# Six places of a fused attention and MLP kernel re-ordered

## The chip, the cores and the metric

The kernel runs on one core of a Trainium2 chip. The metric is the device time of one execution in microseconds (us). The engines are named as in the profile: PE (TensorE, matmuls), PEld (its weight loads), DVE (VectorE), ACT (ScalarE), POOL (GpSimd) and SP (SyncE, which here only issues transfers). Each engine works through its own queue in order and waits at an instruction until what that instruction needs is there; everything queued behind it waits too.

## The reference

Two branches read the same input `x` of 2048 tokens by 576 columns (32 heads of 18 columns), and their results are added to it. In the first, a token attends to itself and to seven earlier tokens, two apart. The second mixes neighbouring tokens, and then has an MLP of width 4608.

```python
def A(xn, wqkv, wo):                      # W, dil = 8, 2
    q, k, v = heads(xn @ wqkv)
    logits = einsum("bhsd,bhswd->bhsw", q, k[idx]) * scale   # idx = pos - 2 * (0..7), masked below 0
    return merge(einsum("bhsw,bhswd->bhsd", softmax(logits), v[idx])) @ wo

def B(x, w1, w2, w3, w4):
    h = gelu(layernorm(x) @ w1)
    x1 = x + shifted(h) @ w2              # four column blocks shifted by +1, -1, +2, -2 tokens
    return x1 + gelu(layernorm(x1) @ w3) @ w4

xn = layernorm(x)
return x + A(xn, wqkv, wo) + B(xn, w1, w2, w3, w4)
```

## The kernel before

Everything is float32. Each product is made from operands split in two parts: a *hi* part, a copy that ACT casts to the matmul's input type (fp32r), and a *lo* part, the difference between the value and hi, which DVE computes. `split_*`, `cast_*`, `hi_main`, `lo_main`, `signed` and `low_part` are these steps, for weights, for transposed tokens, for gelu results. A cast by ACT is therefore nearly always followed by a difference on DVE that reads ACT's result, and PE needs both.

The order of the instructions on each engine is the order in which the Python code emits them. Waits between engines follow from which tile is read or written, and a tile that is used again waits until its earlier users are done. The stages, in order of time:

**Prologue** (up to 24 us). The first four tiles of 128 tokens (t = 0 to 3) are normalized, turned by PE into a PSUM tile (`turn_x`, L333; the last columns by `turn_tail`, L302) and cast out of it (`cast_x`, L337: ACT L311 and DVE L312 for the main part, ACT L316 and DVE L317 for the tail). `q_part` (L388) issues matmuls n0 to n1 of the 14 of a tile's first product, `q_tail` the last two, and `q_leave`, which takes the result out. `split_cg(3)` splits the second block of weights, `rawb`, that later products use. The tiles are done in turn, and "unit 4", the first product with the second block, follows.

**Steps of q, k and v** (to about 192 us). Blocks p = 3 to 7 are made by a Strassen-like scheme, seven products of sums instead of eight. Each p has numbered slots, and a plan says which side work is emitted after which slot. `z_turn(t)` (L556) scales a tile on ACT (L558) and turns it on DVE (L129, L130); `put` stores the turned block. The matmuls are in `seven` (L593); `leave` (L601) takes a product out, with a copy on ACT or an addition on DVE (L608).

**The mixing branch** (to about 310 us), then **units** u = 0 to 23 (to about 613 us). A unit is a quarter of the tokens by 256 of the MLP's width: two `up` products (L1128, matmuls L1132, gelu on ACT L1114, low part on DVE L1126) and four `down` products of the unit before. A `down` (L1159, matmuls L1168) has twelve matmuls in a PSUM tile. The result leaves in one of three ways: a copy on ACT (L1173) and an accumulating transfer by POOL for tiles in `YD`; for a *seeded* tile, where the running sum was copied into PSUM beforehand by ACT (`ahead`, L1149), a copy back by ACT (L1176); otherwise an addition on DVE (L1179). `begin_downs` takes the list of tiles with their flag for seeds. There are two PSUM tiles, and `ahead` prepares the next as soon as one is out. `split_n(b, ...)` (L899) makes the signed hi and lo parts of the normalized block b, after `get_n` has read it by transfer (ACT L906 and following).

**Groups** q = 0 to 23 (to about 1197 us). The rest of the MLP is again Strassen-like. A group has seven products P1 to P7 (matmuls L1430), eight downs D0 to D7 of the group before, and side work. `ORDER` and `ORDERS` give the order of these fifteen items; `at(item, f, ...)` puts `f` behind an item. P3 gives, by the addition `z_add` (L1440), the value whose gelu is `c12` (`gelu12`, L1120; `low12`, L1126); P7 gives `c22` (`gelu22`, `low22`). `combine` (L1260, DVE L1265) makes four sums of weights in place, `split_a` and `split_s` split weights and their sums for the products of the next group, `split_op` the tokens' operands, `load_pair` and `load_w4` read weights. NWP is 12: groups 0 to 11 work on one half of the tokens, 12 to 23 on the other.

The attention runs through units and groups as background work on DVE and ACT. It is a generator; `bg(us, late)` (L1081) is called after each item and takes operations from it, for as much time as the item's other work on DVE (`spent`) has left. With `late` it also emits a pending exponential (`exp_now`). In group 18, behind P4, a loop takes all that is left.

**End.** The eight downs of the last group, then the output product `mm_tok` (L180, matmuls L183), for which `split_wo` splits the weights, and the stores.

Of the kernel before, what the change touches and what calls it, by code (L numbers as in the profile page):

```python
# [8 lines left out]
F32 = mybir.dt.float32  # L9
F32R = mybir.dt.float32r  # L10
AF = mybir.ActivationFunctionType
ALU = mybir.AluOpType
# [24 lines left out]
NPL = 6  # L37
# [20 lines left out]
def fused_block(ctx, tc, x, wqkv, wo, w1, w2, w3, w4, out):  # L58
# [393 lines left out]

    def q_head(t):
        pq[t] = psa.tile([128, 512], F32, name="p1", tag="a")
        q_part(pq[t], t, 0, 0, 12)

    def q_tail(t):
# [20 lines left out]
    q_tail(0)  # L478
    q_tail(1)
    pq[2] = psa.tile([128, 512], F32, name="p1", tag="a")  # L480
    q_part(pq[2], 2, 0, 0, 6)
    turn_tail(2, turns[2])
    cast_x(2, True)
    q_part(pq[2], 2, 0, 6, 12)
    turn_x(3)
    cast_x(3)
    turn_tail(3, turns[3])
    cast_x(3, True)
    q_tail(2)
    split_cg(3)  # L490
    q_head(3)
    q_tail(3)
# [163 lines left out]
    for p in range(3, 8):  # L656
# [6 lines left out]
        if n < 8:  # L663
            q4 = 4 * (p - 3)
            for k, t in zip({3: (9, 11, 14, 17), 6: (9, 11, 12, 14)}.get(p, (9, 12, 16, 18)),
                            (q4 + 1, q4 + 2, q4 + 3, q4) if p == 4 else range(q4, q4 + 4)):
                at(k, z_turn, t)
            at({3: 17, 6: 14}.get(p, 18), put, ("z", p - 3))
            if p > 3:
                at(0, norm_x, 2 * n + 1)  # L670
                at(0, tails, 2 * n + 1)
                at(2, stats_x, 2 * n)
            at(3, low2, n)
            at(4, norm_x, 2 * n)
            at(4, tails, 2 * n)
            at(7, up2, n)
            at(8, lambda n=n: cast_upper(n, two[n]))
            if n < 7:
                at(11, stats_x, 2 * n + 3)
            at(14, cast_s, n, 0)  # L680
            at(15, cast_s, n, 1)
            at(15, cast_s, n, 2)
            if p == 3:
                for t, k in enumerate((9, 11, 14)):
                    at(k, away, t, t + 1)
                at(11, scales, 4, 6)
                at(18, load_x, 13)
                at(18, load_x, 12)
            if p == 4:
                for t, k in ((5, 9), (6, 12), (7, 16)):  # L690
                    at(k, away, t, t + 1)
                at(18, away, 3, 5)
                at(11, scales, 8)
                at(12, scales, 10)
                at(18, load_x, 15)
                at(18, load_x, 14)
            if p == 5:
                at(11, load_w1)
                at(11, scales, 12)
            if p == 6:  # L700
                at(5, scales, 14)
        else:
            at(3, lambda: get(("z", 0), ring_block(("z", 0))))
            at(13, lambda: split_x(xring["z", 0], 2))
            at(15, lambda: split_x(xring["z", 0], 3))
            at(18, open_w1)
            at(18, split_w1, 0)
            at(20, lambda: split_x(xring["z", 0], 1))
# [190 lines left out]
    def split_n(b, xt, part=None, scr=None):  # L899
# [3 lines left out]
        vec = KV[:, b % 2:b % 2 + 1] if b % 2 == 0 else KV[:, 1:2]  # L903
        if part != 1:
            r = xt[:, 9, :] if scr is None else scr.bitcast(F32R)
            act.activation(r[64:128], raw[64:128, 4, :], AF.Identity, scale=k2)  # L906
            act.activation(xt[0:64, 4, :], raw[0:64, 4, :], AF.Identity, scale=k2)
            signed(xt[64:128, 4, :], raw[64:128, 4, :], k2, r[64:128])
            act.activation(xt[:, 0:2, :], raw[:, 5:7, :], AF.Identity, scale=k1)
            signed(xt[:, 5:7, :], raw[:, 5:7, :], k1, xt[:, 0:2, :])  # L910
        if part != 0:
            for k, sg in ((2, vec), (3, k2)):
# [346 lines left out]

    def combine(q):  # L1260
        spent[0] += 2.2
        st = WS["st", q]
        for o, i, op in ((1, 0, ALU.subtract), (0, 2, ALU.add), (2, 1, ALU.subtract),
                         (3, 2, ALU.subtract)):
            dve.tensor_tensor(st[:, :, o, :], st[:, :, o, :], st[:, :, i, :], op=op)  # L1265
# [43 lines left out]
    for u, (c, b) in enumerate(units):  # L1309
# [18 lines left out]
        for i in range(C):  # L1328
# [12 lines left out]
            if (u, i) == (3, 0):  # L1341
                pool.dma_start(yd[13], Y[:, 13, :])
                pool.dma_start(yd[15], Y[:, 15, :])
            if (u, i) in ((1, 0), (2, 1)):
                split_n(u + 1, x1n[u + 1], 0, RT)
# [17 lines left out]
        for j, (t, parts) in enumerate(prev):  # L1363
# [6 lines left out]
            if (u, j) == (3, 1):  # L1370
                next(state["gen"])
            if u in (1, 2) and j == 1:
                split_n(u + 1, x1n[u + 1], 1, RT)
            for f in {(-3, 1): (lambda: split_a(0),), (-3, 2): (lambda: split_w4(NPL),),
# [31 lines left out]
        if u in XADD:  # L1406
            add_x(XADD[u])
    close_ab()


    qpcc = tc.tile_pool(name="qpc", bufs=1, space=PSUM, reuse_waits="tile")
    qpc = qpcc.__enter__()
    qpdc = tc.tile_pool(name="qpd", bufs=1, space=PSUM, reuse_waits="tile")
    qpd = qpdc.__enter__()
    begin_downs([(4 * units[NU - 1][1] + j, False) for j in range(4)]
                + [(8 * (g // NWP) + (j + 4) % 8, g + 1 not in (NWP - 1, NWP))
                   for g in range(2 * NWP) for j in range(8)], 2,
                lambda n: qpd.tile([128, 2, 512], F32, name=f"ps{n % 2}"))
    Z1, Z2, Z3, Z4 = temp(13), temp(15), temp(5), temp(7)
    NQ = 2 * NWP  # L1420
    SLOT = {"A11": 0, "A22": 1, "A12": 2, "S1": 0, "S3": 1, "S2": 2, "S4": 3}
# [20 lines left out]
    def downs(g):  # L1442
        s0 = 8 * (g // NWP)
        w1, w0 = W4[2 * (NPL + pair(g))], W4[2 * (NPL + pair(g)) + 1]
        for j in range(8):
            if j < 4:
                yield lambda j=j: down(s0 + 4 + j, [(hid[g, "c12"], w0), (hid[g, "c22"], w1)])
            else:
# [36 lines left out]
    def o_turn(t):  # L1485
# [4 lines left out]
    ORDER = "P1 D0 P2 P6 D1 P5 D2 P7 D3 P4 D4 P3 D5 D6 D7"  # L1490
    ORDERS = {0: "P1 P2 D0 P6 P5 P7 D1 D2 P4 D3 P3",
              NWP - 1: "P1 D0 P2 P6 P5 P7 D1 P4 P3 D2 D3 D4 D5 D6 D7",
              NWP: "D0 D1 P1 D2 P2 P6 D3 P5 P7 D4 P4 P3 D5 D6 D7"}
    spent[0] = 0.0
    for q in range(NQ):
# [36 lines left out]
        if q == 0:  # L1532
            at("P6", split_op, 0, "T4")
            at("D1", gelu22)
            at("P7", split_a, n, (0, 1))
            at("D1", split_op, 0, "B22")
            at("D1", split_a, n, (2,))
            at("D2", low22)
            at("P3", gelu12)
            at("P3", combine, n)  # L1540
            at("P3", low12)
            at("P3", split_s, n, (0, 1))
            at("P3", split_s, n, (2,))
            at("P3", load_pair, q + 2)
        elif q == NWP - 1:
# [16 lines left out]
        elif q == NWP:  # L1562
# [10 lines left out]
            at("P7", split_a, n, (2,))  # L1573
            at("P7", combine, n)
            at("D4", gelu22)
            at("P4", low22)
            at("D5", gelu12)
            at("D5", split_s, n, (0, 1))
            at("D6", low12)
            at("D6", split_s, n, (2,))  # L1580
            at("D7", load_pair, q + 2)
# [15 lines left out]
        else:  # L1597
# [4 lines left out]
            at("D6", low12)  # L1602
            for k, it in enumerate(("P4", "D4", "P3", "D5", "D6")):
                at(it, split_wo, k)
# [7 lines left out]
        if z < -1 and q + 1 != NWP:  # L1612
            at("D5" if q else "P3", load_w4, NPL + pair(q + 1), 0)
        if 0 < q < 9:
# [13 lines left out]
        for it in ORDERS.get(q, ORDER).split():  # L1628
# [40 lines left out]
            for f in plan.get(it, ()):  # L1669
                f()  # L1670
            if z < -6 or z == -6 and EV[0]:
                bg(1.5 - spent[0], it == "P6" and q != NWP - 1)
                spent[0] = 0.0
# [96 lines left out]
```

## Time and profile before

| | |
|---|---|
| median of 3 runs | 1276.82 us (1276.55 to 1279.03) |
| profiled execution | 1276.11 us |
| its span | 1274.3 us |
| PE busy | 1256.3 us (99%) |
| DVE busy | 930.9 us (73%) |
| ACT busy | 765.7 us (60%) |
| POOL busy | 267.9 us (21%) |

In the timeline a row gives the start, the duration, the engine, the line and operation, the output and inputs by the program's names, the shapes, and how many instructions are run together in the row (x). A bracket at its end is the time that the engine stood idle just before, and what released it. In a row of windows there are, after the stretch's length, the busy time of PE, PEld, DVE, ACT and POOL with their instructions, then the granted clock of PE, the share of the transfers' engines, and GB/s.

### The profile page before, as it was taken

The page shows a single profiled execution, that of the slowest core. Times are in us where ns is not written, and L with a number is a line of the kernel's source. Part 1 is how long each engine was busy: PE and PEld are TensorE (multiplying, and loading weights), DVE is VectorE, ACT ScalarE, POOL GpSimd, SP SyncE. Part 2 cuts the span into 40 slices and gives each one's busy share as a digit, 9 for nine tenths or more (in the row PEclk, how much of TensorE's full clock was granted, in tenths as well). Part 3 has the DMA queues.
Part 4 walks back from the last instruction along what each step waited for, and adds up shares of the span by engine and source line. Part 5 has one row for each costly group of instructions (what it writes and reads, how often), then busy time and mean ns, then how long its engine had stood idle before and what let it go on. Part 6 is the DMA issues. An engine that isn't in the chain of part 4 may idle for free.

```text
span 1274.3 us, 21006 instructions
## 1 busy us (share of the span) xinstructions
PE 1256.3 (99%) x7819; PEld 1157.6 (91%) x7819; DVE 930.9 (73%) x1204; ACT 765.7 (60%) x1277; POOL 267.9 (21%) x408
## 2 busy tenths in 40 slices
PE   8999999999999999999999999999999999999998
PEld 8999998899898999999899999998888999898998
DVE  7877645688558989997659998889889883464341
ACT  4455557526645545455777767776677776677730
POOL 2213200021222211212123232222122222222200
PEclk9999999999999999999999999999999999999999
DMA  7638994446878986859669889788968769899972
GB/s 220 155 85 200 224 196 146 149 137 190 203 223 181 221 164 137 162 130 252 120 144 209 189 179 217 179 168 209 249 99 188 144 117 197 182 215 211 267 244 84
DMA packets 208654, 228.92 MB, mean 180 GB/s; under 512 B 80920, under 2 KB 142328, under 8 KB 208424
## 3 DMA queue, kind: packets, MB, share of 16 engines
q1 hardware_dynamic: 175800, 160.79, 44.7%
q0 software_dynamic: 32752, 66.80, 32.5%
q8 instruction: 61, 1.00, 0.3%
q14 instruction: 41, 0.34, 0.1%
HBM read 127.71 MB, written 110.23 MB: 187 GB/s over the span
## 4 chain that ended last, share of the span: by engine, by line
PE 64%; issue 3%; ACT 2%; DVE 2%; DMA 1%; POOL 0%; DVEq 0%; POOLq 0%; ACTq 0%
PE ps L1168 31%; PE cc L1430 19%; PE p L1132 10%; PE ps L183 4%; DMA yd<-Y 1%; DVE xt L897 0%; DVE w3st L1265 0%; POOL yd L1174 0%; ACT Y L1173 0%; PE p L1737 0%; ACT xt L1227 0%; ACT Y L1115 0%; DVE c L1126 0%; DVE Y L1179 0%; ACT c L1120 0%
## 5 line engine op out<-in xcount | busy, mean ns | idle before, releaser
L1168 PEld LDWEIGHTS ps<-w,c 128*128 128x128 f32 x3456 | 479.0, 189 | 22.2 <-ACT Y L1173 2.0
L1168 PE MATMUL ps<-w,c 128*128 128x288 f32 x3456 | 490.0, 297 | 6.2 <-ACT ev L1173 1.5
L1174 POOL DMA_DIRECT2D yd<-Y x154 | 138.0, 899 | 396.3 <-ACT Y L1173 332.0
L1126 DVE TENSOR_TENSOR c<-Y,c 128x512 fp32r<-128x512 f32 x144 | 98.8, 687 | 93.2 <-ACT Y L1115 91.8
L1173 ACT COPY Y<-ps 128x576 f32<-128x576 f32 x154 | 97.8, 636 | 77.2 <-PE ps L1168 66.7
L1430 PE MATMUL cc<-xt,w3s 128*128 128x512 f32 (+1 forms) x504 | 127.7, 393 | 0.9 <-DVE Y L1440 0.9
L1430 PEld LDWEIGHTS cc<-xt,w3s 128*128 128x128 f32 (+1 forms) x504 | 92.2, 188 | 19.1 <-DVE Y L1440 1.4
L1176 ACT COPY Y<-ps 128x576 f32<-128x576 f32 x92 | 58.9, 640 | 66.7 <-PE ps L1168 65.2
L1430 PE MATMUL cc<-x1n,w3a 128*128 128x512 f32 (+1 forms) x336 | 86.4, 396 | 0.3 <-ACT cc L1633 0.3
L1046 DVE TENSOR_TENSOR po<-q,k 128x1152 f32<-128x1152 f32 (+1 forms) x48 | 84.3, 1755 | 0.8
L1049 DVE TENSOR_REDUCE L<-po 128x64 f32<-128x1152 f32 (+1 forms) x48 | 84.0, 1751 | 0.8
L1114 ACT ACTIVATE c<-p 128x512 fp32r<-128x512 f32 x48 | 28.6, 597 | 84.9 <-PE p L1132 84.9
L1440 DVE TENSOR_TENSOR Y<-cc,Y 128x512 f32<-128x512 f32 x49 | 33.7, 688 | 58.9 <-ACT Y L1436 54.5
L1022 DVE TENSOR_TENSOR po<-v,L 128x1152 f32<-128x1152 f32 x56 | 75.4, 1354 | 0.9
L393 PE MATMUL p<-wb,xt 128*128 128x288 f32 (+1 forms) x504 | 71.2, 299 | 1.0 <-ACT stg L398 0.9
L1430 PEld LDWEIGHTS cc<-x1n,w3a 128*128 128x128 f32 (+1 forms) x336 | 61.2, 190 | 11.8 <-ACT cc L1633 0.5
L393 PEld LDWEIGHTS p<-wb,xt 128*128 128x128 f32 (+1 forms) x504 | 67.8, 189 | 2.4 <-ACT stg L398 1.3
L1026 DVE TENSOR_TENSOR po<-po 128x1152 f32<-128x1152 f32 x49 | 66.4, 1355 | 0.9
L597 PE MATMUL ca<-wb,xt 128*128 128x288 f32 x420 | 61.6, 297 | 1.5 <-DVE keep L608 1.5
L1149 ACT COPY ps<-Y 128x576 f32<-128x576 f32 x92 | 59.4, 646 | 4.4 <-DVE Y L1179 2.4
L597 PEld LDWEIGHTS ca<-wb,xt 128*128 128x128 f32 x420 | 57.6, 189 | 2.2 <-DVE keep L608 2.0
L113 POOL TENSOR_TENSOR rs<-rs,mhalf 128x1 f32<-128x1 f32 x32 | 19.4, 606 | 189.7 <-DVE mv L116 109.4
(256 smaller groups left out, 2146.9 us busy)
## 6 DMA issues: line engine op xcount, KB each, us to landing
yd<-Y POOLq DMA_DIRECT2D x156, 288.0 KB, 6.1
Y<-in_B_w_dram SPq DMA_DIRECT2D x29, 576.0 KB, 6.0
w3st<-in_B_w_dram SPq DMA_DIRECT2D x56, 256.0 KB, 8.0
qkvd<-stg SPq DMA_DIRECT2D x66, 144.0 KB, 3.3
yd<-ev POOLq DMA_DIRECT2D x26, 288.0 KB, 6.8
w3st<-in_B_w_dram SPq DMA_DIRECT2D x92, 64.0 KB, 7.8
xd<-st SPq DMA_DIRECT2D x16, 320.0 KB, 5.0
xd<-big SPq DMA_DIRECT2D x16, 320.0 KB, 7.1
```

What stands on the lines that cost most here:

```text
L393: pe.matmul(ps[:, :QB], xo[:n, o + k, a, :], W[:n, w + k, v, :], start=i == 0, stop=i == len(PLAIN) - 1)
L597: pe.matmul(ps[:, :QB], xo[:n, XO[x], a, :], W[:n, OP[w], v, :], start=start and i == 0, stop=stop and i == len(HALVES) - 1, skip_group_ch ...
L1022: dve.tensor_tensor(dst, vv, Lf[:, :, w:w + 1].to_broadcast([128, TPP * GH, HD]), op=ALU.mult)
L1026: dve.tensor_tensor(o, o, dst, op=ALU.add)
L1046: dve.tensor_tensor(dst, qf[:, None, :].to_broadcast([128, n, TPP * GC]), win, op=ALU.mult)
L1049: dve.tensor_reduce(Lw[:, w:w + n, :], dst.rearrange("p w (x d) -> p w x d", d=HD), axis=AX.X, op=ALU.add)
L1126: dve.tensor_tensor(h[:, 1, :], g, h[:, 0, :].bitcast(F32), op=ALU.subtract)
L1132: pe.matmul(ps, W3[f][:, w, :], x1n[b][:, a, :], start=n == 0, stop=n == len(PAIRS) - 1)
L1168: pe.matmul(ps[:, k, :HF], h[:, col], w[:, p, k * HF:(k + 1) * HF], start=n == 0 and not seed, stop=n == len(seq) - 1, skip_group_check=True)
L1173: act.copy(e.rearrange("p (h c) -> p h c", h=2), ps[:, :, :HF])
L1174: pool.dma_start(yd[t], e, accum_op=ALU.add)
L1430: pe.matmul(ps, WX[w][:k, v, SLOT[w], :], area[sb][xk][:k, a, :], start=onto is None and i == 0, stop=last and i == len(HALVES) - 1, skip_ ...
```

## The change

It moves work in six places; no matmul is added or removed.

1. In the prologue, `split_cg(3)` is taken apart: its hi and lo parts are emitted between the casts of tiles 2 and 3, the rest behind the tail cast of tile 3. `q_tail(2)` and the first six matmuls of tile 3 come ahead of `turn_tail(3)`.
2. For p = 6, the third and fourth `z_turn` go from slots 12 and 14 to 13 and 15, the `put` from 14 to 15.
3. `split_n` gets two more parts: 2 is the block's tail (with its lo), 3 the first two main pieces. For unit 2's block these and part 1 are emitted behind the downs 0, 1 and 2 of unit 1, where part 0 had stood behind the first `up` and part 1 behind down 1. Unit 3's block stays as it was.
4. In group 0, P3 comes ahead of D3, and the side work is placed anew, with `combine` in two halves.
5. In group 12, `combine` and `split_s` are halved in another place, and `bg` is skipped behind P6; the pending exponential is emitted behind P3 instead.
6. The last group's eight downs have no seeds (three of them had), and `split_wo` is spread differently. In addition the first four downs of all groups take `c22` first and `c12` second.

```diff
+    r3, o3 = qraw[3], OP["B12"]
     pq[2] = psa.tile([128, 512], F32, name="p1", tag="a")
     q_part(pq[2], 2, 0, 0, 6)
+    hi_main(r3, 0, o3, 0)
     turn_tail(2, turns[2])
     cast_x(2, True)
+    hi_main(r3, 0, o3, 1)
+    lo_main(r3, 0, o3, 0)
     q_part(pq[2], 2, 0, 6, 12)
     turn_x(3)
     cast_x(3)
+    q_tail(2)
+    lo_main(r3, 0, o3, 1)
+    pq[3] = psa.tile([128, 512], F32, name="p1", tag="a")
+    q_part(pq[3], 3, 0, 0, 6)
     turn_tail(3, turns[3])
     cast_x(3, True)
-    q_tail(2)
-    split_cg(3)
-    q_head(3)
+    split_tail(r3, 0, o3)
+    q_part(pq[3], 3, 0, 6, 12)
     q_tail(3)
...
-            for k, t in zip({3: (9, 11, 14, 17), 6: (9, 11, 12, 14)}.get(p, (9, 12, 16, 18)),
+            for k, t in zip({3: (9, 11, 14, 17), 6: (9, 11, 13, 15)}.get(p, (9, 12, 16, 18)),
...
-            at({3: 17, 6: 14}.get(p, 18), put, ("z", p - 3))
+            at({3: 17, 6: 15}.get(p, 18), put, ("z", p - 3))
...
-        if part != 1:
+        if part not in (1, 3):
             r = xt[:, 9, :] if scr is None else scr.bitcast(F32R)
...
+        if part not in (1, 2):
             act.activation(xt[:, 0:2, :], raw[:, 5:7, :], AF.Identity, scale=k1)
             signed(xt[:, 5:7, :], raw[:, 5:7, :], k1, xt[:, 0:2, :])
-        if part != 0:
+        if part not in (0, 2, 3):
...
-    def combine(q):
-        spent[0] += 2.2
+    def combine(q, n0=0, n1=4):
+        spent[0] += 0.55 * (n1 - n0)
...
-                         (3, 2, ALU.subtract)):
+                         (3, 2, ALU.subtract))[n0:n1]:
...
-            if (u, i) in ((1, 0), (2, 1)):
+            if (u, i) == (2, 1):
                 split_n(u + 1, x1n[u + 1], 0, RT)
...
-            if u in (1, 2) and j == 1:
-                split_n(u + 1, x1n[u + 1], 1, RT)
+            if u == 1 and j < 3:
+                split_n(2, x1n[2], (2, 3, 1)[j], RT)
+            if (u, j) == (2, 1):
+                split_n(3, x1n[3], 1, RT)
...
-                + [(8 * (g // NWP) + (j + 4) % 8, g + 1 not in (NWP - 1, NWP))
+                + [(8 * (g // NWP) + (j + 4) % 8, g + 1 not in (NWP - 1, NWP, NQ))
...
-                yield lambda j=j: down(s0 + 4 + j, [(hid[g, "c12"], w0), (hid[g, "c22"], w1)])
+                yield lambda j=j: down(s0 + 4 + j, [(hid[g, "c22"], w1), (hid[g, "c12"], w0)])
...
-    ORDERS = {0: "P1 P2 D0 P6 P5 P7 D1 D2 P4 D3 P3",
+    ORDERS = {0: "P1 P2 D0 P6 P5 P7 D1 D2 P4 P3 D3",
...
         if q == 0:
-            at("P6", split_op, 0, "T4")
+            at("D0", split_op, 0, "T4")
+            at("P6", split_op, 0, "B22")
+            at("P7", split_a, n, (0, 1))
             at("D1", gelu22)
-            at("P7", split_a, n, (0, 1))
-            at("D1", split_op, 0, "B22")
             at("D1", split_a, n, (2,))
-            at("D2", low22)
+            at("D1", combine, n, 0, 2)
+            at("D2", combine, n, 2, 4)
+            at("P3", split_s, n, (0,))
             at("P3", gelu12)
-            at("P3", combine, n)
-            at("P3", low12)
-            at("P3", split_s, n, (0, 1))
-            at("P3", split_s, n, (2,))
-            at("P3", load_pair, q + 2)
+            at("P3", low22)
+            at("D3", low12)
+            at("D3", split_s, n, (1, 2))
+            at("D3", load_pair, q + 2)
...
-            at("P7", combine, n)
+            at("P7", combine, n, 0, 2)
+            at("D4", combine, n, 2, 4)
             at("D4", gelu22)
             at("P4", low22)
             at("D5", gelu12)
-            at("D5", split_s, n, (0, 1))
+            at("D5", split_s, n, (0,))
             at("D6", low12)
-            at("D6", split_s, n, (2,))
+            at("D6", split_s, n, (1, 2))
...
-            for k, it in enumerate(("P4", "D4", "P3", "D5", "D6")):
+            for k, it in enumerate(("P4", "D4", "P3", "P3", "D7")):
                 at(it, split_wo, k)
...
-            at("D5" if q else "P3", load_w4, NPL + pair(q + 1), 0)
+            at("D5" if q else "D3", load_w4, NPL + pair(q + 1), 0)
...
-            if z < -6 or z == -6 and EV[0]:
-                bg(1.5 - spent[0], it == "P6" and q != NWP - 1)
+            if (z < -6 or z == -6 and EV[0]) and (q, it) != (NWP, "P6"):
+                bg(1.5 - spent[0], it == "P6" and q != NWP - 1 or (q, it) == (NWP, "P3"))
```

More of the change, by code (lines that the diff above doesn't have):

```diff
@@ L451, in fused_block @@
     pq = {t: psa.tile([128, 512], F32, name="p1", tag="a") for t in range(2)}
-    def q_head(t):
-        pq[t] = psa.tile([128, 512], F32, name="p1", tag="a")
-        q_part(pq[t], t, 0, 0, 12)
     def q_tail(t):
@@ L1408, in fused_block @@
     close_ab()
+    NQ = 2 * NWP
     qpcc = tc.tile_pool(name="qpc", bufs=1, space=PSUM, reuse_waits="tile")
@@ L1419, in fused_block @@
     Z1, Z2, Z3, Z4 = temp(13), temp(15), temp(5), temp(7)
-    NQ = 2 * NWP
     SLOT = {"A11": 0, "A22": 1, "A12": 2, "S1": 0, "S3": 1, "S2": 2, "S4": 3}
```

## The prediction

> **What bounds the kernel now.** I read the page's first two lines, then the timeline of TensorE (PE) filtered for idle in front of an instruction, then for each such idle the other engines' rows around it.
>
> ```profile
> span 1274.3 us, 21006 instructions
> PE 1256.3 (99%) x7819; PEld 1157.6 (91%) x7819; DVE 930.9 (73%) x1204; ACT 765.7 (60%) x1277; POOL 267.9 (21%) x408
> ```
>
> PE is busy all but 1274.3 - 1256.3 = 18.0 us, and the change removes no matmul. Only those 18 us, and matmuls that run slowly, can be won. An edit that makes ACT or DVE shorter where PE does not wait is worth nothing. So I looked where PE stands still in the six places:
>
> ```profile
> 18.28 0.41 PE L304 MATMUL ps<-ident,stg 128*128 128x128 f32 x2 [1.49 <-DVE xt L312]
> 165.66 0.54 PE L597 MATMUL ca<-wb,xt 128*128 128x288 f32 x2 [1.09 <-DVE keep L608]
> 329.90 1.87 PE L1168 MATMUL ps<-w,c 128*128 128x288 f32 x12 [1.49 <-ACT ev L1173]
> 634.39 0.80 PE L1168 MATMUL ps<-w,c 128*128 128x288 f32 x4 [0.87 <-ACT c L1120]
> 636.57 2.13 PE L1168 MATMUL ps<-w,c 128*128 128x288 f32 x8 [1.39 <-DVE c L1126]
> 920.91 1.88 PE L1430 MATMUL cc<-xt,w3s 128*128 128x512 f32 x7 [0.95 <-DVE Y L1440]
> 924.82 3.46 PE L1168 MATMUL ps<-w,c 128*128 128x288 f32 x24 [0.42 <-DVE Y L1179]
> 930.11 1.86 PE L1168 MATMUL ps<-w,c 128*128 128x288 f32 x12 [0.21 <-ACT ps L1149]
> 1197.05 5.20 PE L1168 MATMUL ps<-w,c 128*128 128x288 f32 x36 [0.50 <-ACT ps L1149]
> 1203.14 8.26 PE L1168 MATMUL ps<-w,c 128*128 128x288 f32 x60 [0.90 <-ACT Y L1173]
> 337.98 6.55 PE L1168 MATMUL ps<-w,c 128*128 128x288 f32 x48
> ```
>
> The brackets of the ten sum to 9.31 us. A stall costs a little more than its bracket: twelve matmuls of a down take 6.55/4 = 1.64 us in a stream, but 1.87 between two breaks, so 0.23 us drains at each. Ten stalls are worth 9.31 + 10 x 0.23 = 11.6 us. One more item (product or down) is 1.6 us; I use that pitch below.
>
> **Part 1, fourth tile's tails.**
>
> ```profile
> 16.77:19.90 3.13, 1.64 (x14) 1.65 (x14) 1.11 (x2) 1.76 (x4) 0.00 (x0) 1.00 0.02 5
> 16.82 0.58 ACT L311 CAST xt<-ps 128x512 fp32r<-128x512 f32 x1 [0.88 <-PE ps L300]
> 17.44 0.69 DVE L312 TENSOR_TENSOR xt<-ps,xt 128x512 fp32r<-128x512 f32 x1 [1.04 <-ACT xt L311]
> 18.73 0.37 ACT L316 CAST xt<-ps 96x256 fp32r<-96x256 f32 x1 [1.32 <-PE ps L304]
> 19.13 0.42 DVE L317 TENSOR_TENSOR xt<-ps,xt 32x256 fp32r<-32x256 f32 x1 [1.00 <-ACT xt L316]
> 18.45 2.64 PE L393 MATMUL p<-wb,xt 96*128 96x288 f32 x18
> ```
>
> The tail transposes wait until ACT's cast and DVE's difference have read their PSUM tile (18.13); then 2 + 12 + 2 matmuls at 2.64/18 = 0.147 us follow, to about 20.7. The change puts q_tail(2) and the first six of tile 3 (8 x 0.147 = 1.2 us), which need only the cast's end at 17.40, into the gap; what precedes them still waits to 17.44. The transposes keep 18.3. Behind them six matmuls end near 19.5, and the last two need the tail's difference, which ends at 19.55. Tile 3 ends at 19.9: **0.8 us** (0.3 if the weight casts, moved into ACT's 0.88 and 1.32 us holes, push the tail's casts; 1.1 if nothing waits).
>
> **Part 2, z turns.**
>
> ```profile
> 163.17 0.27 DVE L130 STREAM_TRANSPOSE st<-z 128x128 f32<-128x128 f32 x1
> 164.36 0.71 DVE L129 STREAM_TRANSPOSE st<-z 128x512 f32<-128x512 f32 x1 [0.93 <-ACT z L558]
> 165.19 0.42 DVE L608 TENSOR_TENSOR keep<-ca,keep 128x288 f32<-128x288 f32 x1
> ```
>
> The addition L608 stands in DVE's queue behind the transposes of slot 12's z turn, which themselves wait 0.93 us for ACT. Moved to slot 13 they come after it; the addition can follow 163.17 + 0.27, ends at about 163.9, and the stall goes: 1.09 + 0.23 at most, of which I take **1.25** (0.6 if ACT's later queue, one slot fuller, delays a copy). The `put` is one slot later on SP; nothing waits for that store in PE's rows, so nothing.
>
> **Part 3, second unit's casts.**
>
> ```profile
> 326.14 0.63 ACT L906 ACTIVATE Y<-x1n 64x512 fp32r<-64x512 f32 x1 [2.15 <-DMA x1n<-xn]
> 328.28 0.57 ACT L1114 ACTIVATE c<-p 128x512 fp32r<-128x512 f32 x1
> 329.23 0.62 ACT L1173 COPY ev<-ps 128x576 f32<-128x576 f32 x1
> 339.29 0.63 ACT L906 ACTIVATE Y<-x1n 64x512 fp32r<-64x512 f32 x1
> 341.55 0.62 ACT L1173 COPY Y<-ps 128x576 f32<-128x576 f32 x1
> ```
>
> ACT stands 2.15 us at L906 for unit 2's tile to land; the gelu (328.28) and the copy that frees the PSUM tile (329.23) queue behind. With the casts behind the downs these run as PE delivers: the 1.72 us stall goes. But unit 3's casts stay where they are, behind a transfer whose landing at 339.29 does not move, while PE is 1.72 us earlier. The copy at 341.55 therefore stays, ends at 342.17, and it frees the tile of the fourth down, which would start at 337.98 + 3 x 1.64 - 1.72 = 341.2: about 1.1 us comes back. Net **0.6** (1.75 if the transfer moves too; -0.7 if a split cast comes too late for unit 2's first matmul as well, about the 0.63 of one cast and a drain).
>
> **Part 4, first group's last product.**
>
> ```profile
> 632.99 0.68 DVE L1440 TENSOR_TENSOR Y<-cc,Y 128x512 f32<-128x512 f32 x1
> 633.59 2.33 DVE L1265 TENSOR_TENSOR w3st<-w3st 128x384 f32<-128x384 f32 x4
> 633.70 0.63 ACT L1120 ACTIVATE c<-Y 128x512 fp32r<-128x512 f32 x1
> 635.83 0.69 DVE L1126 TENSOR_TENSOR c<-Y,c 128x512 fp32r<-128x512 f32 x1
> 633.40:636.80 3.40, 1.14 (x6) 0.79 (x6) 3.02 (x6) 2.37 (x4) 0.87 (x1) 1.00 0.41 47
> 636.80:640.20 3.40, 3.40 (x12) 3.03 (x12) 1.92 (x2) 3.37 (x7) 0.77 (x1) 0.50 0.41 59
> 640.20:643.60 3.40, 3.40 (x20) 2.97 (x19) 0.69 (x1) 1.82 (x4) 0.00 (x0) 1.00 0.54 161
> ```
>
> P3 is the group's last item, so the next down waits for P3's sum, then c12's gelu (0.87), then the low part, which DVE does only after 2.33 us of weights' sums (1.39). With P3 ahead of D3, sums at D1 and D2, and c22 first, gelu and low part have D3 and P1 (3.2 us) as cover; the chain 0.68 + 0.63 + 0.69 needs 2.0. If that cover were gone the 1.4 would be back. So 2.26 + 2 x 0.23 = 2.7 goes. And the windows show a second loss: right after 3.40 us with PE busy for 1.14, the clock is 0.50 for 3.4 us, with 12 matmuls where the next window has 20: half of the stretch, 1.7 us. Without the idle I expect it not to happen. With 0.2 for a shorter wait of P1, **4.6** (2.6 to 4.8). The later load_pair and load_w4 (one item, 1.6 us, on SP) are not waited for in any row here.
>
> The Trainium skill (TensorE: Matmul & The Clock Gate, "What's actually happening") says that the clock goes to half only after a whole idle window of about 3.4 us. By that rule the gaps here would not be the cause, and the second loss would stay. The trace had no such idle, only 0.87 and 1.39 us, and yet shows 0.50; so I side with the trace, and keep the rule as a rival. The stretch from 16.77 had 1.64 of 3.13 us busy and kept 1.00: the limit, if it is one, lies below that share.
>
> **Part 5, weights' sums halved.**
>
> ```profile
> 929.41 0.64 ACT L1149 COPY ps<-Y 128x576 f32<-128x576 f32 x1
> ```
>
> Four sums in a row (2.33 us, as at 633.59) hold DVE ahead of L1179; skipped background work frees DVE ahead of L1440 too. The three stalls are 1.58 + 3 x 0.23 = 2.3 us; but the next group's first down then asks for its seed at 927.9, earlier than ACT can give it (PE being 1.4 earlier, ACT's queue the same): I leave 0.5 and a drain. **1.45** (2.0 if the seed comes as early as PE; 0.6 if the first of them, 0.95 + 0.23, comes back in half).
>
> **Part 6, last group without seeds.**
>
> ```profile
> 1202.46 0.63 ACT L1173 COPY Y<-ps 128x576 f32<-128x576 f32 x1
> ```
>
> Each unseeded down saves two ACT copies (0.64 as in 929.41, 0.63) and adds 0.75 us of DVE, which has room at the end. The copy at 1202.46, for which PE waits 0.90, is ahead by the seeds that stood before it; the 0.50 goes. 1.40 + 2 x 0.23 = 1.86, plus some 0.15 of a wait inside the first row, less 0.36 that the copy for the second of these downs still costs: **1.65** (2.0 without that copy's wait; 0.8 if the new additions or the moved weight casts let one such wait of 0.90 stand).
>
> **Sum.** 0.8 + 1.25 + 0.6 + 4.6 + 1.45 + 1.65 = 10.35. The profiled execution took 1276.11, of which 1274.3 is span; its time is 0.71 under the median of the runs. 1276.11 - 10.35 = 1265.8; by the median 1276.82 - 10.35 = 1266.5. I say 1266.3. All low ends: 0.3 + 0.6 - 0.7 + 2.6 + 0.6 + 0.8 = 4.2, so 1272.6; all high ends 12.95, so 1263.9.
>
> **Rivals.**
>
> ```profile
> 482.00:578.00 96.00, 96.00 (x573) 87.43 (x572) 94.19 (x83) 51.45 (x82) 17.24 (x20) 1.00 0.67 138
> 1036.00:1067.00 31.00, 31.00 (x185) 27.84 (x184) 18.09 (x22) 21.83 (x35) 8.69 (x11) 1.00 0.74 137
> 1046.98 1.35 DVE L1026 TENSOR_TENSOR q<-q,po 128x1152 f32<-128x1152 f32 x1
> 1065.05 1.90 PE L1430 MATMUL cc<-xt,w3a 128*128 128x512 f32 x7
> ```
>
> (a) The half clock comes anyway: 1.7 less, 1268.0. For it the rule, against it the windows; 0.12.
>
> (b) What parts 1 to 3 win (2.65) is eaten in the attention stretch, where DVE is busy 94.19 of 96 us and PE, arriving earlier, would begin to wait for it: 1276.8 - 7.7 = 1269.1. Against it: PE is busy 96.00 of 96 there, with no wait yet. 0.08.
>
> (c) Slower: the attention's place. Background work skipped in group 12 pushes DVE's attention operations later, and in group 18, behind P4, a loop issues in one go whatever is left. The last one is at 1046.98, that P4 at 1065.05, 18 us later; one skip is one operation (1.35 us). Should ten or more be left there, 10 x 1.35 = 13.5 us of DVE would stand in front of what PE needs, and eat the 10.35: it decides from eight. With ten, 1280. The 31-us window shows DVE idle for 12.9 us, room for nine, so this is unlikely: 0.07.
>
> (d) No change: waits go by whole tiles, and a reader of a tile that is now written in two parts still waits for the later one, so that each stall stays or comes back an item later: 1276.5; 0.05.
>
> The forecast itself gets 0.68. The range must hold it, its unknown ends, (a) and (b): 1263.4 to 1272.2. About 0.2% (2.55 us) is what a measurement of this kernel can tell from no change: faster 0.88, same 0.05, slower 0.07.
>
> **What would show it.** Right: the ten brackets gone or small; 1.00 clock at 637; small waits left near 17, 341, 928 and 1201. Wrong: part 3, if unit 3's casts start well before 339; part 4, if 0.50 stands near 635 without an idle; part 5 or 6, if a bracket over 0.5 us stands in front of a down behind a seed copy. The forecast as a whole is wrong if new brackets beyond 2 us in all stand in places that had none.

## The result

The changed kernel takes 1268.72 us (median of 4 runs, 1268.14 to 1269.61) against 1276.82 before: 8.1 us less, a ratio of 0.9933 with a 95% interval of 0.9916 to 0.9951. Run again later, beside another kernel, it took 1267.63 (6 runs, 1266.44 to 1269.03) against 1277.36, a ratio of 0.9922 (0.9909 to 0.9936). 1266.3 was forecast, in a range from 1263.4 to 1272.2.

The first lines of the page of the changed kernel:

```profile
span 1266.4 us, 20999 instructions
PE 1254.4 (99%) x7819; PEld 1156.8 (91%) x7819; DVE 933.0 (74%) x1207; ACT 761.6 (60%) x1271; POOL 266.9 (21%) x408
```

The span is 7.9 us shorter. PE's busy time has fallen by 1.9, about what the stretch at half clock had cost; the rest is idle that went. Its timeline, where PE still waits in the six places, and where it starts the down that had waited longest:

```profile
18.30 1.07 PE L393 MATMUL p<-wb,xt 128*128 128x288 f32 x6 [0.41 <-ACT xt L311]
164.81 1.63 PE L600 MATMUL ca<-wb,xt 128*128 128x288 f32 x11
329.75 6.19 PE L1136 MATMUL p<-x1n,w3a 128*128 128x512 f32 x26 [0.53 <-DVE x1n L900]
630.84 1.76 PE L1172 MATMUL ps<-w,c 128*128 128x288 f32 x12
635.92 0.50 PE L1436 MATMUL cc<-xt,w3s 96*128 96x512 f32 x1 [0.33 <-DMA w3s<-w3st]
902.47 1.89 PE L1436 MATMUL cc<-x1n,w3a 128*128 128x512 f32 x7 [0.93 <-ACT cc L1641]
922.15 1.86 PE L1172 MATMUL ps<-w,c 128*128 128x288 f32 x12
927.63 0.50 PE L1436 MATMUL cc<-xt,w3s 96*128 96x512 f32 x1 [0.53 <-DMA w3s<-w3st]
936.43 1.89 PE L1436 MATMUL cc<-xt,w3a 128*128 128x512 f32 x7 [0.28 <-ACT Y L1442]
1195.17 8.27 PE L1172 MATMUL ps<-w,c 128*128 128x288 f32 x60 [0.60 <-ACT Y L1177]
```

The ten brackets of before are gone or smaller. The rows at 635.92 and 927.63 are new: one matmul that waits for a transfer into `w3s`. So are 0.53 in front of unit 2's first product and 0.28 at 936.43; these four sum to 1.67 us. The wait at 902.47 has grown from 0.29 to 0.93. The window that had 1.14 of 3.40 us busy, and the slow one behind it, read now (the clock is the third number from the end):

```profile
630.20:633.60 3.40, 3.40 (x22) 3.06 (x21) 2.52 (x3) 3.37 (x7) 1.66 (x2) 1.00 0.38 33
633.60:637.00 3.40, 3.07 (x16) 2.35 (x15) 0.69 (x1) 2.05 (x4) 0.00 (x0) 1.00 0.43 74
637.00:640.40 3.40, 3.40 (x22) 3.10 (x21) 0.00 (x0) 1.24 (x3) 0.89 (x1) 1.00 0.88 249
```

Since both kernels issue the same 7819 matmuls, the difference between the two starts of the n-th matmul says how far ahead the changed kernel is at that point. Its steps, from the two traces:

| place | forecast | measured step |
|---|---|---|
| first 11 us, ahead of every edit | 0 | -0.85 |
| part 1, at 18 us | +0.8 | +0.82 |
| part 2, at 166 | +1.25 | +1.40 |
| part 3, at 330 | +1.72 - 1.1 | +0.80 |
| part 4, 629 to 636 | +4.6 | +4.64, then -0.60 |
| c22 first, 897 to 903 | 0 | +0.35, then -0.64 |
| part 5, 913 to 943 | +1.45 | +1.90, then -0.79 and -0.28 |
| part 6, 1189 to 1196 | +1.65 | +0.75 and +0.42 |

(These sum to 7.9, the difference of the two spans.) The first row is a start at which the loads of `x` and of the first weights landed 0.4 to 1.0 us later. In other profiles, of kernels with the same prologue, PE was between 0.7 us earlier and 0.4 later there, so it is scatter.

### The profile page after: what moved, and what is told of

It is laid out like the page before. It is cut to its first block, busy times and chain, and to the rows that moved or that the text cites. A ratio compares the mean times of both kernels' runs of the same rounds, so it can differ in the third digit from the quotient of the medians.

```text
span 1266.4 us, 20999 instructions
## 1 busy us (share of the span) xinstructions
PE 1254.4 (99%) x7819; PEld 1156.8 (91%) x7819; DVE 933.0 (74%) x1207; ACT 761.6 (60%) x1271; POOL 266.9 (21%) x408
## 4 chain that ended last, share of the span: by engine, by line
PE 42%; issue 5%; DMA 2%; POOL 1%; ACT 1%; DVE 0%; POOLq 0%; ACTq 0%
PE ps L1172 20%; PE cc L1436 18%; PE ps L183 4%; DMA yd<-Y 1%; POOL yd L1178 1%; DMA w3s<-w3st 1%; PE p L1745 0%; DVE w3st L1269 0%; ACT Y L1177 0%; POOL w3s L1296 0%; ACT xt L1240 0%; ACT w3s L1274 0%; ACT cc L1641 0%; ACT Y L1442 0%; POOL w3a L1287 0%
```

## The experiments

Steps of this kind ("PE falls behind", "gains") are from here on against the first profile of the changed kernel, by equal counts of matmuls.

**tails_early.** One theory for the missing part of 4 and 5: what was moved was not only DVE's part of `split_s`.

```diff
             at("P3", low22)
+            at("P3", split_s, n, (1,))
             at("D3", low12)
-            at("D3", split_s, n, (1, 2))
+            at("D3", split_s, n, (2,))
...
-            at("D5", split_s, n, (0,))
+            at("D5", split_s, n, (0, 1))
             at("D6", low12)
-            at("D6", split_s, n, (1, 2))
+            at("D6", split_s, n, (2,))
```

> The changed kernel, but in groups 0 and 12 the tail step of split_s (an ACT pass, then POOL's accumulating transfer into w3s) stands one item earlier. Theory (the missing gain of parts 4 and 5 went into a new wait for that transfer, which was moved one item back): the idle of 0.33 us at 635.9 and of 0.53 at 927.6, released by the transfer into w3s, go, each with 0.23 of drain; about 1.2 us faster than the changed kernel, near 1267.5. Rival (the transfer only lands when the reads of weights beside it let it, so an earlier issue doesn't land earlier): both idles stay within 0.2 us, time 1268.7.

1268.51 us (4 runs, 1266.91 to 1269.03), no difference that such runs can show; 1267.5 was expected. By place it is as expected at both transfers: +0.56 at 635.9 and +0.81 at 927.6, and no bracket is left there. POOL's rows, first of the changed kernel and then of this one, show that the order of two transfers has changed as well:

```profile
631.12 0.86 POOL L1178 DMA_DIRECT2D yd<-Y  x1 [5.16 <-ACT Y L1177]
631.81 0.97 POOL L1296 DMA_DIRECT2D w3s<-w3st  x1
```

```profile
632.21 0.78 POOL L1296 DMA_DIRECT2D w3s<-w3st  x1 [5.14 <-PE cc L1436]
632.86 1.05 POOL L1178 DMA_DIRECT2D yd<-Y  x1
```

In the changed kernel the transfer into `w3s` was issued behind that of a down's result (`yd`) and took 4.1 us to landing; issued ahead of it, it took 2.5. Against PE's own progress the issue was only 0.7 us earlier, so more than half of what it gained is a quicker landing. At 923 it is the same: 4.5 us behind a `yd` transfer, 2.5 ahead of it.

But in group 12 ACT's pass for the tail now stands ahead of a seed copy, and the next down waits for that (0.54 lost):

```profile
923.00 1.87 PE L1172 MATMUL ps<-w,c 128*128 128x288 f32 x12 [0.73 <-ACT ps L1153]
```

In its profile a further 0.65 went at the last group's fourth down, which no edit touched (1.26 us idle instead of 0.60).

**low_repeats.** The dispute on the clock by itself: idles of four sizes, made by repeating one DVE operation, which changes no value.

```diff
             at("D6", low12)
+            for _ in range({19: 6, 20: 8, 21: 10}.get(q, 0)):
+                at("D6", low12)
...
             at("D3", low12)
+            for _ in range(4):
+                at("D3", low12)
```

> The changed kernel with the low part of c12 computed again and again (the same values), to hold PE at the next group's first down: 4 extra in group 0, 6, 8 and 10 extra in groups 19, 20 and 21, 0.62 to 0.69 us each. Slack before PE waits: about 1.3 us in group 0 and 3.1 in the others, so idles of about 1.2, 0.8, 2.0 and 3.2 us. Theory (the half clock came from the two idles together, PE busy 1.14 of 3.40 us): 0.50 for 3.4 us follows where the idle leaves PE under about 1.2 to 1.6 us busy in 3.4, so after group 20 and 21, not after 19, perhaps not in group 0. Rival by the Trainium skill (only a whole idle window of about 3.4 us): at most after group 21. Rival (it has nothing to do with idles): after none.

The timeline's four waits, and windows of the stretch with each idle and, for the last two, of the stretch behind it:

```profile
634.64 0.53 PE L1172 MATMUL ps<-w,c 128*128 128x288 f32 x2 [1.54 <-DVE c L1130]
1099.90 0.53 PE L1172 MATMUL ps<-w,c 128*128 128x288 f32 x2 [1.18 <-DVE c L1130]
1127.17 0.53 PE L1172 MATMUL ps<-w,c 128*128 128x288 f32 x2 [2.64 <-DVE c L1130]
1157.46 0.53 PE L1172 MATMUL ps<-w,c 128*128 128x288 f32 x2 [4.09 <-DVE c L1130]
```

```profile
632.00:635.40 3.40, 1.86 (x13) 1.59 (x12) 3.30 (x5) 1.78 (x5) 1.56 (x2) 1.00 0.66 86
635.40:638.80 3.40, 3.40 (x18) 2.85 (x18) 1.62 (x3) 2.54 (x5) 0.00 (x0) 1.00 0.43 96
1124.20:1127.60 3.40, 0.76 (x6) 0.53 (x5) 3.26 (x6) 0.62 (x2) 0.00 (x0) 1.00 1.03 245
1127.60:1131.00 3.40, 3.40 (x10) 2.62 (x10) 1.72 (x5) 1.58 (x3) 0.00 (x0) 0.50 1.09 295
1158.30:1161.70 3.40, 3.40 (x10) 2.63 (x9) 1.31 (x3) 2.14 (x4) 0.00 (x0) 0.50 0.76 201
```

Idles of 1.18 and 1.54 us kept 1.00; 2.64 and 4.09 were each followed by 3.4 us at 0.50. In the order of the rows PE fell 1.79, 1.53, 4.46 and 5.92 us behind: the idle plus 0.25 to 0.35 without the drop, plus 1.8 with it. So it is the idle, not the place, and the drop costs about 1.5 us where 1.7 was reckoned. (One time, 1283.34 us, longer by the idles.)

Where the windows that count begin can be read from the traces' record of the clock. It begins at 5.32 us in the kernel before, at 4.62 here and at 4.46 in group0_only below, and each stretch at 0.50 starts a whole number of 3.413 us later: 185 of them at 636.78 in the kernel before, 329 and 338 here, 96 at 332.14 in group0_only. So the windows stand still, and an idle counts by how much of it falls into one. On that grid, in all twelve traces, every window with 1.43 us busy or less was followed by one at 0.50, and none with 1.73 or more was. The idle of 4.09 us shows it best: it was shared by two windows, and the clock fell only at 1158.32, when PE had been at work again since 1157.46.

```profile
1151.50:1154.91 3.41, 1.87 (x13) 1.55 (x11) 3.24 (x6) 1.57 (x3) 0.86 (x1) 1.00 1.05 249
1154.91:1158.32 3.41, 0.86 (x5) 0.77 (x6) 3.31 (x7) 0.24 (x1) 0.00 (x0) 1.00 1.09 244
```

An idle window as a whole, as the Trainium skill has it (TensorE: Matmul & The Clock Gate, "What's actually happening": about 3.4 us), was not needed: 2.64 us in one piece was enough here, as 2.26 in two was.

**seeds_and_bg_back.** Which of the edits in parts 5 and 6 carry them.

```diff
-                + [(8 * (g // NWP) + (j + 4) % 8, g + 1 not in (NWP - 1, NWP, NQ))
+                + [(8 * (g // NWP) + (j + 4) % 8, g + 1 not in (NWP - 1, NWP))
...
-            if (z < -6 or z == -6 and EV[0]) and (q, it) != (NWP, "P6"):
-                bg(1.5 - spent[0], it == "P6" and q != NWP - 1 or (q, it) == (NWP, "P3"))
+            if z < -6 or z == -6 and EV[0]:
+                bg(1.5 - spent[0], it == "P6" and q != NWP - 1)
```

> The changed kernel with the last group's seeds back and with background work behind P6 of group 12 as before. Theory (each of the two edits carries most of its part's gain): idles at the last group's first and fourth downs come back, about 1.1 us lost behind 1188; and 0.95 us with a drain in front of P3 of group 12, about 1.2 us lost near 913. Rival (the order of split_wo, and the halved sums, carry the gains): under 0.3 us lost at each place.

```profile
913.86 1.89 PE L1436 MATMUL cc<-xt,w3s 128*128 128x512 f32 x7 [0.96 <-DVE Y L1446]
1196.62 8.27 PE L1172 MATMUL ps<-w,c 128*128 128x288 f32 x60 [0.90 <-ACT Y L1177]
```

1.23 us lost near 913, as the theory has it, and 0.20 + 0.67 in the last group, where about 1.1 was expected: the idle at the fourth down is back, at the first down there is no bracket. One time of 1269.61 us, in a profile whose start was 0.5 earlier.

**wo_sums_casts.** Three others.

```diff
-            for k, it in enumerate(("P4", "D4", "P3", "P3", "D7")):
+            for k, it in enumerate(("P4", "D4", "P3", "D5", "D6")):
...
-            at("P7", combine, n, 0, 2)
-            at("D4", combine, n, 2, 4)
+            at("P7", combine, n)
...
-            if u == 1 and j < 3:
-                split_n(2, x1n[2], (2, 3, 1)[j], RT)
+            if u == 1 and j < 2:
+                split_n(2, x1n[2], j, RT)
```

> The changed kernel with three other places undone or altered, far apart: split_wo spread as before; the weights' sums of group 12 in one piece; unit 2's tail and first casts together behind the first down and the rest behind the second. Theory: the sums in one piece hold L1183 and bring back an idle of about 0.4 us near 917 (0.65 with the drain); the old spread of split_wo loses under 0.2 us; the casts one down earlier end the 0.53 us idle at 329.75, so 0.5 to 0.75 gained there. Rivals: the sums lose nothing, the skipped background work having made room for them; the casts earlier push ACT's copies of the downs and gain nothing.

The sums in one piece lose 0.63 at 917 (an idle of 0.38 behind L1183), as expected, but 0.40 is back at the next seed copy: halving them is worth 0.2. The spread of `split_wo` moves nothing measurable. The casts one down earlier gain 0.94 at 329.75, of which 0.21 goes at 340.7. (1267.98 us, one time.)

**group0_only.** Part 4 alone, put into the kernel before, with c12 first.

> The kernel before with the new order and plan of group 0 alone, c12 still first in the downs. Theory: the two idles of 0.87 and 1.39 us and the half clock behind them go, and the new idle for the transfer into w3s comes (0.3 with a drain of 0.23); PE is 3.6 to 4.0 us ahead of the kernel before from group 1 on, and the end is that much earlier: 1276.8 - 3.8 = 1273.0. Rival (the half clock belongs to the place, not to the idle): 0.50 still stands near 636, 2.0 to 2.2 us ahead, 1274.7. Rival (the order c22 first is what makes it): the next group's first down still waits over 0.5 us for c12's low part.

1274.06 us (10 runs) against 1277.55, a ratio of 0.9967 (0.9955 to 0.998): 3.5 us. From group 1's first product to its second down PE gains 4.64 us on the kernel before and gives 0.73 back, 3.91 in all; there is no idle at the first down, and the transfer's in its place:

```profile
641.64 0.50 PE L1430 MATMUL cc<-xt,w3s 96*128 96x512 f32 x1 [0.46 <-DMA w3s<-w3st]
```

Yet at the end of its profile PE is only 0.62 ahead of the kernel before. It started 0.6 later, lost more before 323 where nothing was edited, and 2.0 us at unit 2's casts, which this kernel has as before. There the wait was 1.98 us instead of 1.49, and the clock fell:

```profile
331.76 2.96 PE L1168 MATMUL ps<-w,c 128*128 128x288 f32 x12 [1.98 <-ACT ev L1173]
328.73:332.14 3.41, 1.43 (x11) 1.19 (x11) 2.50 (x4) 3.41 (x6) 0.00 (x0) 1.00 0.85 210
332.14:335.55 3.41, 3.41 (x15) 3.22 (x14) 1.88 (x3) 1.87 (x4) 0.00 (x0) 0.50 0.38 77
```

The ten runs differ in this too. Five have a mean granted clock of 1.000 and take 1271.93 to 1273.74 us; five have 0.999, as one stretch of 3.4 us at 0.50 makes it, and take 1274.38 to 1276.23.

**tails_and_turns_back.** Parts 1 and 2 undone in the changed kernel (the code of before in both places).

> The changed kernel with part 1 (fourth tile's tails) and part 2 (z turns of p = 6) undone. Theory (what is won early is carried to the end): PE falls 0.8 us behind the changed kernel at 18 us and a further 1.3 to 1.4 at 166, and stays 2.1 to 2.2 behind to the end, apart from 0.5 either way that the landing of transfers moves from run to run. Rival (the attention stretch, where DVE is busy nearly throughout, or waits for transfers level this out): under 1 us behind from 600 us on.

PE loses 0.81 at 18 us and 1.28 at 166, with the brackets of before (1.49 and 1.09). But it gets 0.95 back at 329.75 and 0.74 at 902, loses 0.4 and 0.27 between these, and ends 0.7 behind. (Its start was 0.9 earlier, and 0.7 went before 318 where nothing was edited.) Neither number is met: PE is 1.3 behind in the attention stretch and 1.3 to 1.6 from 600 to 898, mostly less than the theory's 2.1 with its margin of 0.5, and more than the rival's 1; only behind 902 is it under 1. The attention stretch gives nothing back. The two places that do are waits for transfers, told below. 1268.87 us (one time).

**c12_first.** The order of the two parts in all downs undone.

```diff
-  yield lambda j=j: down(s0 + 4 + j, [(hid[g, "c22"], w1), (hid[g, "c12"], w0)])
+  yield lambda j=j: down(s0 + 4 + j, [(hid[g, "c12"], w0), (hid[g, "c22"], w1)])
```

> The changed kernel with the downs of all groups taking c12 first again. Theory (the new order of group 0 is enough, and in group 12 the gain of c22 first is taken back by the wait for a staging tile's transfer at 902): no idle over 0.2 us at group 1's first down; PE 0.3 to 0.5 behind at 897, level again behind 902.5; time as the changed kernel within 0.5 us. Rival (c22 first carries a share of part 4): an idle of 0.4 us or more near 631 and over 0.6 us lost for good.

No bracket at group 1's first down. 0.43 lost until 898 and 0.63 back at 902.5, where PE's wait is 0.30 instead of 0.93. So c22 first is worth nothing that these runs can show. (1269.03, one time; this profile had also lost 1.1 us near 186, where PE waited for an ACT copy, and 0.4 at the start, in places the edit doesn't touch.)

**combined, combined2.** What the runs so far point to: the edits of tails_early, the casts of wo_sums_casts, and for the last group (the comments give what differs in combined2)

```diff
-            EV[0] = (9, 11, 10, 15, 13)
-        if j in (0, 2):
-            split_x(xo[0], j // 2)
+            k = evc[0] + 1
+            EV[0] = [(15, 13, 9, 11, 10)[(m - k) % 5] for m in range(5)]
+        if j in (1, 2):                       # combined2: if j in (2, 4):
+            split_x(xo[0], j - 1)             # combined2: j // 2 - 1
```

> The changed kernel with what the runs so far point to: the tail step of split_s one item earlier in groups 0 and 12, unit 2's tail and first casts together behind the first down, and in the last group staging tiles that no transfer is still reading (15 and 13 first) with split_x behind the second and third down instead of the first and third. By the traces: 0.56 + 0.27 + 0.7, and 0.6 + 0.23 in the last group if both the staging tile and the casts ahead of the copy made its idle: 2.3 us less than the changed kernel, about 1266.4. If only one of the two made it, the other is within 0.2 us of it and the idle shrinks by less than 0.3: 1267.0.

1268.87 us (6 runs): no gain. The wait at the fourth down went, and a longer one came at the fifth. DVE's queue in its timeline says why:

```profile
1195.91 1.23 DVE L156 TENSOR_TENSOR x1n<-x1n 128x1024 fp32r<-128x1024 f32 x1 [0.90 <-ACT x1n L155]
1197.05 0.75 DVE L1183 TENSOR_TENSOR Y<-ps,Y 128x576 f32<-128x576 f32 x1
```

The third down's addition (L1183) could have run at 1194.6; it stands behind `split_x`'s difference, which waits for ACT. I had priced ACT's queue and not DVE's. Hence:

> As combined, but in the last group split_x stands behind the third and the fifth down, after each one's addition on DVE. combined had no idle at the fourth down (the staging tile was free), but 1.7 us at the fifth, because split_x's differences stood in DVE's queue ahead of the third down's addition. Theory (each wait is set by what is queued ahead): both idles go, 0.6 to 0.85 us less than the changed kernel behind 1195, and the end is 1.5 to 2.0 us earlier in all with the other edits' 0.6, 0.3 and 0.4; 1267.0. Rival (split_x is now too late for the output product): an idle of over 0.5 us in front of the first matmuls of L183 near 1203, time as the changed kernel.

1266.14 us (6 runs, 1265.53 to 1267.44), 0.9911 of before (0.9897 to 0.9925). The changed kernel in the same series took 1267.63. In the last group PE runs through without a bracket, a gain of 0.86:

```profile
1188.70 13.10 PE L1172 MATMUL ps<-w,c 128*128 128x288 f32 x97
1201.63 4.56 PE L183 MATMUL ps<-Wo,x1n 128*128 128x288 f32 x33
```

So the fastest version is 1.5 us ahead of the changed kernel by the medians, though single runs of the two overlap (1266.44 to 1269.03 there). Its places sum to nearly as much: +0.93 at unit 2's casts and -1.40 at unit 3's (below), +0.61 and 0.82 - 0.55 at the transfers, +0.86 in the last group, 1.3 us.

**changed_again.** The unaltered changed kernel beside it.

> The changed kernel once more, unaltered, on the same chip as combined2: 1268.7 within 1 us. It also shows what moves between two profiles of one kernel. Theory (transfers land at times of their own and level PE out at unit 2's casts near 330 and at the staging tile near 902): where PE comes to 315 us later than in the first profile, the idle at 329.75 is smaller by about as much, and at 902 likewise. Rival (the differences between profiles are spread evenly): the idle at 329.75 is 0.53 within 0.1 whatever PE's time at 315.

In this profile PE was 0.89 later than in the first at 318 us, and waited 0.7 less at unit 2's casts, as the theory has it. At 902 it was otherwise: PE came later and waited longer, 1.16 us. There ACT's copy of a down's result waits for a transfer that still reads its staging tile, and the next copy, for which PE waits, is queued behind it; in the first profile:

```profile
900.77 0.64 ACT L1177 COPY Y<-ps 128x576 f32<-128x576 f32 x1 [2.99 <-DMA yd<-Y]
```

When that transfer is done scatters, and does not only level. The casts' first instruction on ACT, in the first profile and in this one, with its wait for the read of the block:

```profile
325.66 0.63 ACT L909 ACTIVATE Y<-x1n 64x512 fp32r<-64x512 f32 x1 [2.04 <-DMA x1n<-xn]
```

```profile
325.82 0.63 ACT L909 ACTIVATE Y<-x1n 64x512 fp32r<-64x512 f32 x1 [1.31 <-DMA x1n<-xn]
```

The block lands at the same time within 0.16 us, though PE is 0.89 apart. What PE has won by then is partly waited for here.

## Why the prediction was right, and where its steps were not

**The reading of what bounds it** held: gains came only where PE stood still or its clock was down. Of the 10.35 us, 8.1 and 9.7 were measured in two series. The time alone would not have told the forecast from its rivals: 1268.72 lies nearer to the 1268.0 of (a) and the 1269.1 of (b) than to 1266.3. The gains by place decide.

**Parts 1 and 2** were sized well (0.82 for 0.8; 1.40 for 1.25). What failed is the unwritten step that they reach the end. Part 3 of the prediction held a landing fixed, but counted PE only 1.72 us earlier there, not the 2.05 of parts 1 and 2 as well. Undone, they cost 2.1 at their places, and PE was 0.7 behind at the end (one profile, in which 0.9 and 0.7 of scatter nearly cancel). Rival (b) had the right idea, that an early PE meets another resource, and the wrong one: not DVE in the attention stretch, through which the changed kernel's lead stays at 2.21 us from 332 to 628, but transfers, at 330 and 902. In one profile 0.53 was waited for at 330, in another nothing, with PE later.

**Part 3** has nearly the forecast net (0.80 for 0.6) by luck, since the mechanism was another. I held the landing of unit 3's block fixed at 339.29, and named casts well before 339 as the sign of being wrong. They started at 337.60:

```profile
337.60 0.63 ACT L909 ACTIVATE Y<-x1n 64x512 fp32r<-64x512 f32 x1 [0.54 <-DMA x1n<-xn]
```

SP issued the block's read at 331.64 before and at 330.33 now, so the landing was not fixed, and nothing was given back at 341. Instead the split casts came late for unit 2's first product, which I had put only into the low end. In combined2, where that wait is gone, the 341 mechanism appears as predicted: PE arrives 1.06 earlier, and loses 1.40.

```profile
340.79 1.87 PE L1172 MATMUL ps<-w,c 128*128 128x288 f32 x12 [1.13 <-ACT Y L1177]
```

**Part 4** gave what was forecast, 4.64 for 4.6, up to P6 of group 1, and there lost 0.60. The idles and the half clock went, and rival (a) fell with low_repeats. The term for the half clock was right for the profile from which it was read, but it is not the same in every run: of 35 further runs of the kernel before, 7 have a mean granted clock of 1.000, 17 have 0.998 or 0.999 (about one stretch at 0.50) and 11 have 0.997 or less (two or more). All ten runs of the changed kernel have 1.000. The term that was missing: `split_s` has three steps, and the middle one ends in a transfer by POOL. I counted its DVE and ACT work, and wrote of the moved transfers only that nothing waits for `load_pair` and `load_w4`. In the changed kernel its issue (631.81) came behind that of a down's result, and its data landed at 635.88, 4.1 us later. That is 0.33 + 0.23 us; tails_early, which issued it first, gave 0.56 back.

**Part 5** is the same error once more, and larger: 1.90 was won at its stalls, 0.53 + 0.23 lost to the transfer that stands one item later (0.81 by tails_early), and 0.28 at 936.43, whose cause stays open, leaving 0.83. Luck hid part of it: the wait for a seed copy near 928, for which I left 0.5 and a drain, cost only some 0.3 in all (no bracket at 922.15). What carries the gain is the skipped background work (1.23), not the halved sums (0.2).

**Part 6** gave 1.17 for 1.65. The wait that I left at 0.36 was 0.60, and two things made it at nearly one time: ACT's casts of `split_x` ahead of the copy, and its staging tile, from which a transfer still read. ACT's timeline shows the one until 1194.25 and the other in the copy's bracket:

```profile
1193.20 1.05 ACT L155 CAST x1n<-x1n 128x1024 fp32r<-128x1024 f32 x1
1194.48 0.64 ACT L1177 COPY Y<-ps 128x576 f32<-128x576 f32 x1 [0.23 <-DMA yd<-Y]
```

combined2, which changed both, has no wait there; no run tells the two apart. The missing seeds carry 0.87 of the gain, by seeds_and_bg_back.

**Rivals (c) and (d).** The attention's last operation, and the P4 behind which a rest would have been issued:

```profile
1044.49 1.35 DVE L1030 TENSOR_TENSOR q<-q,po 128x1152 f32<-128x1152 f32 x1
1058.28 1.90 PE L1436 MATMUL cc<-xt,w3a 128*128 128x512 f32 x7
```

Nothing was left to drain; the distance is 13.8 us where it was 18.1. Nor did the waits by whole tiles keep any of the stalls.

**The forecast against the profile** is 2.4 us apart: 0.85 the start of this profile, 0.56 part 4, 0.62 part 5, 0.48 part 6 and 0.29 at 897 to 903, less 0.37 that parts 1 to 3 gave more. The range had room for it.

## What to carry to other kernels

Where one engine is busy 99%, list the idles in front of it with what released each: their sum plus a drain apiece, and what a lower clock costs, is the ceiling, and many can be taken out by re-ordering what is queued ahead of the releaser. Then follow the earlier engine to the next thing that keeps its own time, most of all a transfer, since gains made before it may be waited for there. And when a helper is moved, list what it issues on every queue: the moved DVE work was right twice, and twice the one small transfer beside it, now issued behind another, became the new wait.

## What the runs showed of the hardware

TensorE's granted clock went by fixed windows of 3.413 us, counted from where the record of the clock begins. A window with 1.43 us busy or less (group0_only, one idle of 1.98 us) was followed by one at 0.50, which costs some 1.5 us more; a window with 1.73 or more was not (combined, at its idle of 1.69 us):

```profile
1195.43:1198.85 3.42, 1.73 (x13) 1.49 (x12) 2.94 (x3) 1.92 (x3) 1.22 (x2) 1.00 1.07 226
```

Where between the two the limit lies, no run shows. I had expected the two idles of before to be the cause, but not so sharp a step, nor that the same kernel loses it in one run and not in the next. And the small accumulating transfer into `w3s` takes 2.6 us to landing in the median, by the list of transfers, but took 4.1 and 4.5 us (issues at 631.81 and 923.05) at the two places where PE waited for it, each behind a `yd` transfer issued 0.7 and 1.2 us earlier. It took over 4 us at four other issues too, where PE had time and no `yd` transfer stood just ahead; so such a transfer ahead is not all that goes with a late landing:

```profile
w3s<-w3st POOLq DMA_DIRECT2D x23, 64.0 KB, 2.6
631.81 0.97 POOL L1296 DMA_DIRECT2D w3s<-w3st  x1
...
923.05 0.77 POOL L1296 DMA_DIRECT2D w3s<-w3st  x1 [0.36 <-ACT w3s L1276]
```
